# Side-row casts without repeated rows, batch 5 convolved in one phase, and whole side tasks in the first phases of a convolution with a multiplicative feed-forward behind it

## The chip, the cores and the metric

The kernel runs on one core of one Trainium2 chip. TensorE (PE, with its weight loads PEld), VectorE (DVE), ScalarE (ACT) and GpSimd (POOL) compute; SyncE (SP) issues most of the stores and all DMA transpositions; POOL issues the loads that change the type. Each engine works through its own instructions in order. The metric is the device time of one execution in microseconds (us), 539.42 as the median of three runs before the change.

## What is computed

A causal depthwise convolution with 7 taps (softmax weights, one set for each of 8 heads of 24 columns) runs over 8 sequences of 3904 rows and 192 columns; its result goes through a multiplicative feed-forward:

```
w = softmax(weight)                        # 8 heads x 7 taps
y[b, s, h*24+g] = sum_k w[h, k] * xpad[b, s+k, h*24+g]     # six zero rows ahead of each sequence
x  = y.reshape(31232, 192)
a  = x @ w1;  b = x @ w2                   # 192 x 1024 each
out = ((a * b) @ w3) @ w_out               # 1024 x 1024, 1024 x 192
```

The kernel multiplies w3 and w_out once at the start (W_sb, 1024 x 192), so each row needs two products: the first with w1 and w2, the second with W_sb.

## The kernel before, in words

**Rounds and phases.** The 31232 rows are taken as two streams of 15616 rows (NS = 2, four sequences each), and these in 31 rounds of 512 rows (the last one 256). One round does both streams at once: a stream's 64 columns take half of PE's rows. `first_product` (L549) computes for one round eight blocks of 128 features: PE writes `pa` and `pb` (L564), ACT copies `pa` to `asb` (L571), DVE multiplies it with `pb` into `abT` (L573). `second_product` (L583) multiplies `abT` with W_sb (L589), ACT copies the result to `osb` (L594), SP stores it (L599). The main loop (L810) goes in phases, counted from 0 here as in the code: phase p does the first products of one trio of rounds, 3p to 3p+2, then the six second products (n = 0 to 5) of the same trio. Phase 0's first products stand ahead of the loop, with the loads, the W_sb work and the first convolutions between them. So phase 1 holds rounds 3 to 5, phase 4 rounds 12 to 14.

**Two ways to the convolved rows.** Both leave them with columns on partitions.

- The matrix way (17 of the rounds: 0 to 8, 13 to 16, 21 to 24). The input is loaded in windows of 32 rows (`xb`, L158, issued by POOL) in seven batches; batch 3 covers up to round 4, batch 4 rounds 5 to 8, batch 5 rounds 13 to 16, batch 6 rounds 21 to 24. `conv` (L306) multiplies a window with a band matrix on PE (L324), and the result is evicted by ACT or DVE to `convo` (L333). `store` (L340) writes a batch to `rows` in DRAM (SP, L355 and L362), and `transposes` (L392) reads it back transposed to a ring `xT` of four rounds (SP, L396). Batches 4 to 6 are convolved in four units each, a unit being two heads, by `convolve` after one of the second products of a phase; `places` (L694) lists after which. Where a sequence starts inside a batch, POOL clears the six rows ahead of it in `xb` (L831), behind a phase's other POOL work.
- The side way (14 rounds: 9 to 12, 17 to 20, 25 to 30). `side_cast` (L443) copies the input rows of a task (1024 rows, 64 columns, both streams), with 16 rows ahead of them (HALO), to `rows_c` in DRAM in bf16, one DMA on POOL's queue for each stream (L448). `side_transpose` (L454) brings them, columns on partitions, into one of five `raw` tiles in two halves (SP, L457). ACT multiplies the first tap (`side_first`, L462), DVE adds the other six (`side_sums`, L480). Seven half tasks (BY_POOL) are summed by POOL instead (L507, L527, L522), one in each of phases 2 to 8, from a tile that SP transposes (L501) at the end of the phase before.

**The side plan.** The 18 tasks for DVE are dealt to phases in order (L694 to L714): phase p takes sums until `rooms[p]` is used up, so a task may be split over two phases. `starts[p]` are the tasks that begin in phase p; `chain[p]` is the order in which a phase calls `side_first` and the sums, each `side_first` with the earliest n at which it may be emitted. The result before the change: phase 0 does task 0 and three sums of task 1; phase 1 the rest of task 1, task 2, and two sums of task 3; phase 2 the rest of 3, task 4 and one sum of 5; phase 3 the rest of 5 and task 6.

**Order on the queues.** In phase 0 POOL issues (`later_loads`, L735) batch 3's loads, weights, the casts of `starts[0]`, batch 4's loads and the casts of `starts[1]`. SP's order there is: transpositions of `starts[0]`, batch 3's store, xT for rounds 3 and 4 (all L765 and L766), the output stores of the second products, batch 4's store and xT for rounds 5 and 6 (`turn`, L804), the last output store, then the transpositions of `starts[1]`. In the later phases the issues on POOL's queue (`jobs`) are spread over eight points of the first products, each behind a small copy (`pace`, L820) that waits for an `abT` block; a POOL sum stands at seven of these points too. Where a DMA writes rows that an earlier one read, or reads rows that an earlier one wrote, the framework makes it wait.

Of the kernel before, what the change touches and what calls it, by code (L numbers as in the profile page):

```python
# [16 lines left out]
def kernel(  # L17
# [14 lines left out]
    G = D // H  # L32
# [5 lines left out]
    TS = B * S // NS  # L38
# [5 lines left out]
    Q = 64  # L44
# [25 lines left out]
    t0 = (LAG + 3) * CH  # L70
# [26 lines left out]
    def banks(name):  # L97
        return psum.tile([128, NS, CH], FP32, tag="banks", name=name)
# [8 lines left out]
    rows_c = dram.tile([TS, NP, NS * Q], BF16, name="rows_c")  # L107
    taps_d = dram.tile([H, K], FP32, name="taps_d")
    x_rows = x.rearrange("b s d -> (b s) d")


    def shape_of(b):
        n = SIZES[b] // 4
        m = n // (1 if b < 3 else 2)
        return n, m, n // m
# [6 lines left out]
    def group(r, e):  # L122
        return slice((2 * r + e) * C, (2 * r + e) * C + C)
# [55 lines left out]
    for r in range(NS):  # L179
        p = group(r, 0).start  # L180
# [12 lines left out]
        out=diag, in_=diag, pattern=[[-1, 128 + 8]], compare_op=ALU.is_equal,  # L193
# [13 lines left out]
    for i in range(4):  # L207
        d = diag[i * C:i * C + C, i * C + 2 * i:i * C + 2 * i + C]
        nc.vector.tensor_copy(
            out=cmask[i * C:i * C + C],  # L210
            in_=bass.AP(tensor=d.tensor, offset=d.offset, ap=[d.ap[0], [1, 2], [1, C]]))
# [10 lines left out]
    V, A, P = nc.vector.tensor_copy, nc.scalar.copy, nc.gpsimd.tensor_copy  # L222
# [29 lines left out]
    for i in range(3):  # L252
# [3 lines left out]
        out=share[:, :, 0:K], in0=taps.unsqueeze(1).to_broadcast([H, H, K]), scalar=total,  # L256
        in1=diag[0:H, 0:H].unsqueeze(2).to_broadcast([H, H, K]), op0=ALU.mult, op1=ALU.mult)
    spread = banks("spread")
    for i in range(4):
# [6 lines left out]
        out=wsb, in_=spread[:, 0, 0:2 * H].rearrange("p (h k) -> p h k", h=H)  # L266
# [5 lines left out]
        out=cprod.rearrange("p h k (s two) -> p h k s two", two=2),  # L272
# [6 lines left out]
    p = group(1, 0).start  # L279
# [3 lines left out]
    for k in range(2):  # L283
# [5 lines left out]
                          in_=bps[:, 0, 0:C * H].rearrange("p (h s) -> p h s", s=C))  # L289
# [8 lines left out]
    def segments(c0, n):  # L298
        out = []
        while n:  # L300
            m = min(n, Q - c0 % Q)
            out.append((c0 // Q, c0 % Q, m))
            c0, n = c0 + m, n - m
        return out

    def conv(b, c0, wd, evict=(nc.scalar.copy,), es=None):  # L306
        n, m, E = shape_of(b)
        es = range(E) if es is None else es
        if b not in convo_of:
            convo_of[b] = work.tile([128, n, NP, NS, Q], BF16, tag="convo", bufs=2,  # L310
                                    name="convo")
            left_of[b] = D * E
        convo = convo_of[b]
        cps = {e: banks("cps") for e in es}
        c = c0
        while c < c0 + wd:
            h = c // G
            c1 = min(h * G + G, c0 + wd)
            for j in range(4):
                xb, s = xb_of[b][j]  # L320
                for e in es:
                    for r in range(NS):
                        o = cps[e][j * C:j * C + C, r, 0:m * wd]
                        nc.tensor.matmul(  # L324
                            o.rearrange("p (w g) -> p w g", g=wd)[:, :, c - c0:c1 - c0],
                            Aband[group(r, e), h, :], xb[group(r, e), s:s + m, c:c1],
                            start=True, stop=True)
            c = c1
        for f, e in zip(evict, es):
            src = cps[e][:, :, 0:m * wd].rearrange("p r (w g) -> p r w g", g=wd)  # L330
            o = 0
            for k, lo, c in segments(c0, wd):
                f(out=convo[:, e::E, k, :, lo:lo + c]  # L333
                    .rearrange("p w r g -> p r w g"), in_=src[:, :, :, o:o + c])
                o += c
        left_of[b] -= wd * len(es)
        if not left_of[b]:
            del xb_of[b]
# [61 lines left out]
    HALO = 16  # L400
# [15 lines left out]
    def half_of(q, h):  # L416
        t0, t1 = side_span(q)
        return t0 + h * CH, min(t0 + h * CH + CH, t1)
# [3 lines left out]
    for q in SIDE:  # L422
        for k in range(NP):
            left = [h for h in range(2) if (q, k, h) not in BY_POOL]
            if left:
                tasks.append((q, k, half_of(q, left[0])[0], half_of(q, left[-1])[1]))
    side_of, acc_of, raw_of = {}, [], []
    RAW = HALO + 2 * CH

    def side_tiles():  # L430
# [12 lines left out]
    def side_cast(i, task=None):  # L443
        p, k, t0, t1 = task or tasks[i]

        def job(r):
            def run():
                nc.gpsimd.dma_start(  # L448
                    out=rows_c[t0 - HALO:t1, k, r * Q:r * Q + Q],
                    in_=x_rows[r * TS + t0 - HALO:r * TS + t1, k * Q:k * Q + Q])  # L450
            return run
        return [job(r) for r in range(NS)]

# [6 lines left out]
    def side_first(i):  # L460
        p, k, t0, t1 = tasks[i]
        nc.scalar.activation(  # L462
            out=acc_of[i % 2][:, 0:t1 - t0], in_=raw_of[i % 5 - 1][:, HALO - 1:HALO - 1 + t1 - t0],
            func=ACT.Copy, scale=wC[:, k, K - 2:K - 1])

    def side_sums(i):
        p, k, t0, t1 = tasks[i]
        starts = [z for z in range(0, TS, S) if t0 <= z < t1]
        o = t0 - side_span(p)[0]

        def job(d, last):
            def run():
                raw, acc = raw_of[i % 5 - 1], acc_of[i % 2]
                if d == 2:
                    for z in starts:
                        nc.vector.memset(acc[:, z - t0:z - t0 + 1], 0.0)
                for lo, hi in [(t0, t1)] if last else \
                        zip([t0] + [z + d for z in starts], starts + [t1]):
                    a = acc[:, lo - t0:hi - t0]
                    nc.vector.scalar_tensor_tensor(  # L480
                        out=side_of[p][:, k, o:o + t1 - t0] if last else a,
                        in0=raw[:, HALO + lo - t0 - d:HALO + hi - t0 - d],
                        scalar=wC[:, k, K - 1 - d:K - d], in1=a, op0=ALU.mult, op1=ALU.add)
            return run
        size = (t1 - t0) / (2 * CH)
        return [(size, job(d, d == 0)) for d in list(range(2, K)) + [0]]
# [204 lines left out]
    def stage_of(R):  # L691
        return R // TRIO

    places = {0: (1, 2, 3, 4), 2: (1, 3), 3: (0, 1), 4: (2, 4), 5: (1, 3)}  # L694
    rooms = (9, 11, 11, 11, 11, 12, 12, 12, 12)
    starts, chain, room, p = {}, {}, 0, -1
    for i, (q, *_) in enumerate(tasks):
        for cost, f in side_sums(i):
            while room < cost:
                p += 1  # L700
                room = rooms[p]
                at, ends = 0, {}
                starts.setdefault(p, [])
            if not chain or chain[max(chain)][-1][0] != i:
                starts[p].append(i)
                n = max((p == 0) * (3 * len(starts[p]) - 2), -(-ends.get(i - 2, 0) // 2))
                chain.setdefault(p, []).append((i, n, lambda i=i: side_first(i)))
            assert p < stage_of(2 * q + 1)
            room, at = room - cost, at + cost
            chain.setdefault(p, []).append((i, None, f))  # L710
        ends[i] = at
# [62 lines left out]
    jobs = {p: [] for p in range(1, len(phases))}  # L774
# [4 lines left out]
    casts = [(p - 1, f) for p in starts if p > 1 for i in starts[p] for f in side_cast(i)]  # L779
# [3 lines left out]
    for p in jobs:  # L783
        due_now = sum(d <= p for d, _ in casts)
        ahead = max(due_now, min(len(casts), len(points) - len(jobs[p])))
        first = [] if p == 1 else [f for _, f in casts[:due_now]]
        jobs[p] = first + jobs[p] + [f for _, f in casts[len(first):ahead]]
        del casts[:ahead]
    sent = [LAG + 3]
    due = []  # L790

    def convolve(p):
        b, h, n = units.pop(0)
        conv(b, h * G, n * G, (V, A) if p not in chain or (p == 0 and h == 2 * n) else (A, A))
        if h + n == H:
            store(b)
            while sent[0] < len(conv_rounds) and \
                    min((conv_rounds[sent[0]] + 1) * CH, TS) <= spans[b - 3][1]:
                due.append(conv_rounds[sent[0]])
                sent[0] += 1  # L800
            if p == 0:
                turn(0)

    def turn(p):  # L804
        while due and stage_of(due[0]) <= p + 2 and \
                stage_of(conv_rounds[ring_of[due[0]] - RING // CH]) <= p:
            transposes(due.pop(0))

    pace = const.tile([1, 2], BF16)
    for p, (rounds, ends) in enumerate(phases):  # L810
# [3 lines left out]
        at = [[todo.pop(0) for _ in range(min(each, len(todo)))] for _ in points]  # L814
# [29 lines left out]
        for n, (R, r) in enumerate((R, r) for R in ends for r in range(NS)):  # L844
            (last_product if (R, r) == (NR - 1, NS - 1) else second_product)(R, r)
            if n in places.get(p, ()):
                convolve(p)
            side_steps(p, n + 1, state)
# [35 lines left out]
```

## Time and profile before

| what | value |
|---|---|
| runs | 538.75, 539.42, 539.61 us; median 539.42 |
| the profiled execution | 539.89 us, of which its span (first to last instruction) 538.2 us |
| PE busy | 512.4 us, 95% of the span; granted clock 0.974 in the mean |
| DVE, ACT, POOL busy | 444.7, 348.8, 230.6 us |
| DMA | 58.50 MB, 109 GB/s in the mean |

The page also cuts the span in 40 equal slices of 13.45 us; a digit is the busy share in tenths, and PEclk the granted clock of TensorE:

```
PE   9999699399999999994999999999999999999997
PEclk 9999889789999999996999999999999999999999
DMA  9999959975945496599923636897741320040024
```

PE's row has three low digits inside the run: the fifth slice (53.8 to 67.3 us), the eighth (94.2 to 107.6) and the nineteenth (242.2 to 255.6). The phases of the main loop begin, by PE's first L564 matmul of each, at 77.65, 135.70, 183.81, 231.92, 290.05, 338.10, 385.29 and 432.48 us; phase 0's second products begin at 52.58.

### The profile page before, as it was taken

What the parts mean: (1) busy time and instruction counts of PE and PEld (TensorE: products, weight loads), DVE (VectorE), ACT (ScalarE), POOL (GpSimd) and SP (SyncE); (2) the same over time, 40 slices, a digit from 0 to 9 for tenths busy, and PEclk for the clock granted to TensorE, in tenths of its full rate; (3) what the DMA queues carried; (4) which work ended last, traced back from release to release, by engine and by line L of the source; (5) the groups of instructions that cost most, each with busy time, mean ns of one, the idle gap of its engine ahead of it and who ended that gap; (6) DMA issues with size and microseconds to landing.
All of it is one profiled execution on the core that took longest, in us unless ns stands there. A gap on an engine that the chain in (4) does not pass through costs nothing.

```text
span 538.2 us, 13687 instructions
## 1 busy us (share of the span) xinstructions
PE 512.4 (95%) x5764; PEld 342.5 (64%) x5764; DVE 444.7 (83%) x396; ACT 348.8 (65%) x389; POOL 230.6 (43%) x301
## 2 busy tenths in 40 slices
PE   9999699399999999994999999999999999999997
PEld 4447575159557755951587559557755955775597
DVE  7898289479899799982997999899999999999940
ACT  6786377263776677561767776676477467647742
POOL 8866203100496099335731890395088037300000
PEclk9999889789999999996999999999999999999999
DMA  9999959975945496599923636897741320040024
GB/s 139 152 150 177 108 116 233 169 142 137 152 53 93 128 90 71 113 155 179 144 72 118 50 22 133 147 157 109 202 39 14 119 75 2 31 148 1 1 62 147
DMA packets 157273, 58.50 MB, mean 109 GB/s; under 512 B 113055, under 2 KB 157211, under 8 KB 157211
## 3 DMA queue, kind: packets, MB, share of 16 engines
q0 software_dynamic: 71008, 16.90, 34.7%
q1 hardware_dynamic: 86043, 40.62, 32.5%
q8 instruction: 45, 0.74, 0.5%
q14 instruction: 17, 0.14, 0.1%
q10 hardware_dynamic: 160, 0.10, 0.1%
HBM read 34.09 MB, written 34.90 MB: 128 GB/s over the span
## 4 chain that ended last, share of the span: by engine, by line
PE 77%; DMA 11%; POOL 4%; DVE 3%; SPq 1%; ACT 1%; issue 1%; POOLq 0%; ACTq 0%; DVEq 0%
PE ops L589 26%; PE pa L564 25%; PE pb L564 25%; DMA xb<-in_x_dram 3%; DVE acc L480 2%; DMA rows_c<-in_x_dram 2%; DMA xT<-rows 2%; DMA rows<-convo 2%; POOL xb L158 1%; POOL ws L220 1%; POOL w3b L638 1%; DMA wn<-in_moe_w_dram 1%; SPq L362 1%; PE cps L324 1%; SPq L396 1%
## 5 line engine op out<-in xcount | busy, mean ns | idle before, releaser
L573 DVE TENSOR_TENSOR abT<-asb,pb 128x1024 bf16<-128x1024 bf16 x240 | 292.5, 1220 | 54.8 <-ACT asb L571 21.0
L571 ACT CAST asb<-pa 128x1024 bf16<-128x1024 f32 x244 | 247.1, 1013 | 85.4 <-PE pa L564 85.1
L564 PEld LDWEIGHTS <-wn 64*128 64x128 bf16 x1488 | 138.9, 95 | 96.1 <-DMA xT<-rows 15.9
L564 PEld LDWEIGHTS <-ws 64*128 64x128 bf16 x1488 | 129.9, 94 | 73.3 <-issue 6.1
L589 PE MATMUL ops<-W_sb,abT 128*128 128x192 bf16 x1936 | 165.2, 247 | 0.2 <-ACT convo L333 0.2
L589 PEld LDWEIGHTS <-abT 128*128 128x128 bf16 x1936 | 159.9, 98 | 7.0 <-issue 6.8
L564 PE MATMUL pa<-xT,wn 64*128 64x512 bf16 x408 | 113.1, 383 | 16.1 <-DMA xT<-rows 16.0
L564 PE MATMUL pb<-xT,wn 64*128 64x512 bf16 x408 | 113.6, 381 | 0.0
L564 PE MATMUL pa<-xT,ws 64*128 64x512 bf16 x408 | 113.2, 383 | 0.0
L564 PE MATMUL pb<-xT,ws 64*128 64x512 bf16 x408 | 110.3, 381 | 0.1
L594 ACT COPY osb<-ops 128x768 f32<-128x768 f32 (+1 forms) x61 | 48.5, 795 | 84.4 <-PE ops L589 82.6
L820 POOL COPY pace<-abT 1x2 bf16<-1x2 bf16 x56 | 9.8, 175 | 191.6 <-DVE abT L573 172.6
L564 PE MATMUL pb<-side,wn 64*128 64x512 bf16 (+1 forms) x336 | 88.9, 368 | 0.1
L564 PE MATMUL pa<-side,wn 64*128 64x512 bf16 (+1 forms) x336 | 87.3, 369 | 0.0
L564 PE MATMUL pa<-side,ws 64*128 64x512 bf16 (+1 forms) x336 | 87.3, 369 | 0.0
L480 DVE SCALAR_TENSOR_TENSOR acc<-raw,wC,acc 128x1024 f32<-128x1024 bf16 (+2 forms) x70 | 85.1, 1216 | 2.5 <-ACT acc L462 0.5
L564 PE MATMUL pb<-side,ws 64*128 64x512 bf16 (+1 forms) x336 | 85.6, 368 | 0.0
L507 POOL TENSOR_SCALAR tmp<-acc,wC 128x512 f32<-128x512 bf16 x42 | 65.9, 1568 | 1.2
L448 POOL DMA_DIRECT2D rows_c<-in_x_dram x50 | 38.0, 763 | 22.2 <-DMA raw<-rows_c 16.6
L527 POOL TENSOR_TENSOR acc<-acc,tmp 128x512 f32<-128x512 f32 x35 | 44.4, 1268 | 2.9
L158 POOL DMA_DIRECT2D xb<-in_x_dram x50 | 32.6, 657 | 7.2 <-DMA xb<-in_x_dram 4.0
L480 DVE SCALAR_TENSOR_TENSOR acc<-side,wC,acc 128x1024 f32<-128x1024 bf16 (+1 forms) x20 | 25.2, 1261 | 11.2 <-ACT acc L462 10.7
(71 smaller groups left out, 188.8 us busy)
## 6 DMA issues: line engine op xcount, KB each, us to landing
out_dram<-osb SPq DMA_DIRECT2D x54, 384.0 KB
xb<-in_x_dram POOLq DMA_DIRECT2D x16, 240.0 KB, 7.5
rows_c<-in_x_dram POOLq DMA_DIRECT2D x28, 130.0 KB, 5.3
out_dram<-osb SPq DMA_DIRECT2D x12, 192.0 KB
rows<-convo SPq DMA_DIRECT2D x6, 240.0 KB
xb<-in_x_dram POOLq DMA_DIRECT2D x6, 228.0 KB, 5.5
rows_c<-in_x_dram POOLq DMA_DIRECT2D x16, 66.0 KB, 3.4
w3b<-in_moe_w_dram POOLq DMA_DIRECT2D x4, 256.0 KB, 5.0
```

Of the source, the lines that this page charges most:

```text
L158: nc.gpsimd.dma_start(out=tiles[js[0]][0][group(r, e), s:s + w, :], in_=bass.AP(tensor=x.tensor, offset=(r * TS + t - PAD) * D, ap=[[D, C] ...
L220: f(out=wsw[k][Q * h:Q * h + Q, lo:hi], in_=wn[k][Q - Q * h:2 * Q - Q * h, lo:hi])
L448: nc.gpsimd.dma_start(out=rows_c[t0 - HALO:t1, k, r * Q:r * Q + Q], in_=x_rows[r * TS + t0 - HALO:r * TS + t1, k * Q:k * Q + Q])
L480: nc.vector.scalar_tensor_tensor(out=side_of[p][:, k, o:o + t1 - t0] if last else a, in0=raw[:, HALO + lo - t0 - d:HALO + hi - t0 - d], sc ...
L507: nc.gpsimd.tensor_scalar(out=out, in0=pool_raw[0][:, HALO - d:HALO - d + CH], scalar1=wC[:, k, K - 1 - d:K - d], scalar2=None, op0=ALU.mult)
L527: nc.gpsimd.tensor_tensor(out=a, in0=a, in1=tmp[:, lo - t0:hi - t0], op=ALU.add)
L564: nc.tensor.matmul(p[:, r, f * N:f * N + N], w_of(i, k, r)[rs, ft * 128:(ft + 1) * 128], operand(R, k, rs), start=(k == 0), stop=(k == NP ...
L571: nc.scalar.copy(out=asb[:, :, 0:per * N], in_=pa[:, :, 0:per * N])
L573: nc.vector.tensor_tensor(out=ab[:, f0, :, 0:N], in0=asb[:, :, 0:N], in1=pb[:, :, 0:N], op=ALU.mult)
L589: nc.tensor.matmul(ops[:, g // 2, (g % 2) * D:(g % 2) * D + D], ab[:, jt, r, g * 128:(g + 1) * 128], W_sb[:, jt, :], start=(jt == 0), stop ...
L594: nc.scalar.copy(out=osb.rearrange("p (a g) d -> p a (g d)", g=2), in_=ops[:, 0:ng // 2, 0:2 * D])
L820: P(out=pace, in_=abT_of[R][0:1, ft, 1, 0:2])
```

## The change

Five edits, all in how work is ordered:

- A cast starts at its own first row, without the 16 rows ahead of it, where an earlier cast of the same columns and stream ended at that row (`cast_to`).
- `rooms` goes from 9, 11, 11, 11 to 6, 12, 12, 12 in the first four phases. Whole tasks result: phase 0 does task 0; phase 1 tasks 1 and 2; phase 2 tasks 3 and 4; phase 3 tasks 5 and 6. Task 1's casts and transpositions move from `starts[0]` to `starts[1]`, task 3's from `starts[1]` to `starts[2]`.
- `places`: batch 5's four units stand after n = 0, 1, 3, 4 in phase 2, not after 1, 3 of phase 2 and 0, 1 of phase 3. Its store, which follows the last unit, moves with them, and the xT of rounds 13 and 14 to the end of phase 2.
- A `side_first` may be emitted from about half the sums ahead of it in its phase, less one: n = 2 for the second task.
- `jobs`: in each phase batch loads stand ahead of casts (before: the casts due stood first, but in phase 1). In phase 0 the first half of the third and the fourth unit of batch 4 is evicted by DVE (before: of the third only).

```diff
-    side_of, acc_of, raw_of = {}, [], []
+    side_of, acc_of, raw_of, cast_to = {}, [], [], set()
...
         def job(r):
             def run():
+                lo = t0 if (t0, k, r) in cast_to else t0 - HALO
+                cast_to.add((t1, k, r))
                 nc.gpsimd.dma_start(
-                    out=rows_c[t0 - HALO:t1, k, r * Q:r * Q + Q],
-                    in_=x_rows[r * TS + t0 - HALO:r * TS + t1, k * Q:k * Q + Q])
+                    out=rows_c[lo:t1, k, r * Q:r * Q + Q],
+                    in_=x_rows[r * TS + lo:r * TS + t1, k * Q:k * Q + Q])
...
-    places = {0: (1, 2, 3, 4), 2: (1, 3), 3: (0, 1), 4: (2, 4), 5: (1, 3)}
-    rooms = (9, 11, 11, 11, 11, 12, 12, 12, 12)
+    places = {0: (1, 2, 3, 4), 2: (0, 1, 3, 4), 4: (2, 4), 5: (1, 3)}
+    rooms = (6, 12, 12, 12, 11, 12, 12, 12, 12)
...
-                n = max((p == 0) * (3 * len(starts[p]) - 2), -(-ends.get(i - 2, 0) // 2))
+                n = max(p == 0, int(at) // 2 - 1, -(-ends.get(i - 2, 0) // 2))
...
         ahead = max(due_now, min(len(casts), len(points) - len(jobs[p])))
-        first = [] if p == 1 else [f for _, f in casts[:due_now]]
-        jobs[p] = first + jobs[p] + [f for _, f in casts[len(first):ahead]]
+        jobs[p] += [f for _, f in casts[:ahead]]
...
-        conv(b, h * G, n * G, (V, A) if p not in chain or (p == 0 and h == 2 * n) else (A, A))
+        conv(b, h * G, n * G, (V, A) if p not in chain or (p == 0 and h >= 2 * n) else (A, A))
```

## The prediction

> **What bounds the kernel now.** I read the slices of the page first: PE is busy 95% of the span, and only three slices away from the start fall under 9 tenths. So a change can gain what PE loses there and no more. Next I cut the span at the phase borders (the first pa matmul of each phase) and asked for the busy time of each engine in each stretch. Columns: stretch, length, then busy time of PE, PEld, DVE, ACT, POOL with counts, granted clock, DMA share, GB/s.
>
> ```profile
> 52.58:77.65 25.07, 19.98 (x324) 17.88 (x322) 13.59 (x13) 12.46 (x18) 4.02 (x7) 0.86 0.89 113
> 77.65:135.70 58.05, 49.47 (x483) 31.85 (x484) 43.80 (x36) 31.15 (x32) 7.95 (x15) 0.91 1.00 171
> 135.70:183.81 48.11, 48.11 (x546) 32.72 (x548) 43.75 (x35) 34.65 (x38) 27.96 (x34) 1.00 0.61 101
> 231.92:290.05 58.13, 50.75 (x546) 32.41 (x548) 43.26 (x35) 34.71 (x38) 28.07 (x32) 0.91 0.85 142
> 385.29:432.48 47.19, 47.19 (x483) 32.44 (x484) 44.42 (x39) 31.59 (x33) 22.48 (x24) 1.00 0.34 70
> ```
>
> The last row is a full phase without a convolution: 47.19 us, PE never idle. The third has two convolution units: 0.92 more, so a unit costs PE 0.46. Against these, phase 1 (second row) is 58.05 - 47.19 = 10.86 us too long and phase 4 (fourth row, two units) 58.13 - 48.11 = 10.02. The first row holds only the second products of phase 0. Six such products without a convolution took 15.95 us (385.29 - 369.34, in the chain), four units add 1.84, and 25.07 - 17.79 = 7.28 us is lost. In all 28.2 us.
>
> The view of who waited for whom (us in total, times, longest) and the chain that ended last (start, us, what) name the causes:
>
> ```profile
> PE pa L564 <- DMA xT<-rows: 16.0, 3, 8.6
> PE cps L324 <- ACT osb L594: 4.4, 1, 4.4
> ACT acc L462 <- DMA side<-rows_c: 7.4, 1, 7.4
> POOL rows_c L448 <- DMA raw<-rows_c: 16.6, 1, 16.6
> ```
> ```profile
> 55.35 5.55 DMA rows_c<-in_x_dram
> 60.96 2.56 DMA side<-rows_c
> 63.63 1.15 ACT acc L462
> ...
> 67.23 4.28 PE ops L589 x32
> ...
> 89.13 10.96 DMA rows<-convo
> 100.11 6.97 DMA xT<-rows
> ```
>
> In phase 0, ACT stands at L462 until side task 0 is transposed. The second half of that transposition leaves SP at 60.96, when the cast in flight from 55.35 has landed: the cast of task 3, whose 16 halo rows (5616 to 5631, same columns) are the last rows of task 0. Behind ACT's wait stand the evictions, so PE stands too. Phase 1's loss is the wait of round 5 for batch 4's rows, stored late; phase 4's is round 13's wait for batch 5's. SP's timeline shows why batch 4 is late (start, time, line, operation, count):
>
> ```profile
> 64.80 4.93 SPq L362 DMA_DIRECT2D rows<-convo  x8
> 70.34 8.68 SPq L396 DMA_TRANSPOSE xT<-rows  x6
> 79.06 4.45 SPq L599 DMA_DIRECT2D out_dram<-osb  x5
> 83.61 10.40 SPq L362 DMA_DIRECT2D rows<-convo  x6
> ...
> 223.48 7.69 SPq L362 DMA_DIRECT2D rows<-convo  x6
> ```
>
> All of this stands in one queue behind the transposition held to 60.96. The evictions for the first store had ended at 49.74.
>
> **The change part by part.**
>
> *Halo rows left out, task 1 out of phase 0.* Task 0's second transposition now depends on its own casts alone (the built program lists only an older transposition's semaphore there) and can follow the first, issued at 44.12: lands by about 45.3 + 1.3 + 2.6 = 49.2. ACT reaches L462 after its first osb, at 56.24, so 7 us of cover lie over it. Six sums (6 x 1.27) and the two units whose first half DVE now evicts (2 x 1.21) fit in DVE's stage, which holds nine sums now; each sum too many would cost 1.27. Gain: 7.28; phase 1 starts at 70.4. The halo rows themselves are 16 of 1040: nothing. On POOL task 1's two casts move behind batch 4's twelve loads, so these come some 2 us earlier; task 3's two casts move to phase 1.
>
> *Batch 4's store.* SP no longer stands from 45.3 to 60.96, nor issues task 1's two transpositions first. The first store starts at 49.8. It and the six xT transpositions took 64.80 to 79.02, 14.3 us; started at 49.8 that is 64.1, or 67.2 if batch 4's loads slow them as much as phase 1's loads and casts slowed batch 4's store (15.85 us, 83.61 to 99.46, against 12.96 for batch 5's, 223.48 to 236.44: a factor of 1.22). Five output stores follow at 0.89 each, but the fifth waits for the fifth second product (52.58 + 5 x 2.66 + 3 x 0.46 = 67.3) and its eviction (0.80), ready at 68.2, and batch 4's last unit is evicted at 67.7 + 1.2 = 68.9. So the store starts between 69.2 (68.2 and one output store) and 71.7 (67.2 and five). From its start to round 5's first matmul it was 107.12 - 83.61 = 23.5 us; with batch 5's faster store 20.6. Round 5 can start between 89.8 and 95.2. PE wants it two rounds (77.65 to 98.4) after 70.4, at 91.1. A stall of 0 to 4.1 is left, and with it up to 1.4 of slow clock (the stall of 4.4 us was followed by products of 4.28 for 2.75). I take the middle, 92.5: 1.4 of stall and 0.6 of clock, 2.0. Gain: 10.86 - 2.0 = 8.9.
>
> *All four units of batch 5 in phase 2.* PE does the same matmuls. The store's twelve DMAs (13 us of SP) move from phase 3 to the end of phase 2, ahead of one output store, for which nobody waits; then rounds 13 and 14 are transposed (9 us), so xT is there some 25 us before phase 4. Gain: 10.0. ACT gets two more units in phase 2 (3.7 us) and two fewer in phase 3; it is busy 34.65 of 48.11. The new wait is on POOL: the first unit now follows the first second product and needs the zero rows before a sequence's start (L831), which POOL writes after its side sums, and phase 2 has one pair of DMA issues more (seven, as phase 3 has now):
>
> ```profile
> 169.36 0.56 POOL L831 MEMSET xb<- 6x192 bf16 x2
> 219.09 0.56 POOL L831 MEMSET xb<- 6x192 bf16 x2
> ```
>
> Six pairs: done at 169.92, 34.22 after the phase began. Seven pairs: 219.65 - 183.81 = 35.84. PE reaches the unit at 166.94 - 135.70 + 2.75 = 33.99. So PE waits 1.85, with five second products and their evictions behind it. Slow clock after it: between 0 and 1.85/4.4 of 1.53, 0.6; I take 0.3, since the wait is under half the shortest one that the rows show. Cost 2.2. [...]
>
> *Casts behind the loads, whole tasks.* In phases 2 to 4 the casts go out three points later. Their transpositions serve sums a phase later, some 50 us of cover. Phases 1 to 3 get 12 sums of DVE instead of 11; phase 7 (last row above) already has 12 and loses nothing; without that cover each sum is 1.27. Phase 1's first task is now transposed behind batch 4's store, but 3 us or more before the second products; if that cover went, ACT would wait at L462 as in phase 0, where 7.4 cost PE 7.3. POOL's 16.6 us wait (a cast over rows that task 2's transposition still reads) goes too; nothing on PE hung on it.
>
> Sum: 539.89 (the profiled execution; its span is 538.2) - 7.28 - 8.86 - 10.02 + 2.15 = 515.9. The profiled execution is 0.47 over the median of 539.42, so 515.4; I say 515.5.
>
> **Rivals.**
>
> *Nothing left over:* round 5 finds its tiles and the zero rows come in time: 539.4 - 28.2 = 511.2. For it: the low bounds above. Against it: seven pairs on POOL took what they took.
>
> *The store moves into the loads' time and crawls.* From 49.8 the first store and six transpositions share the DMA engines with the last of batch 4's loads and four casts, and the DMA share from 52.58 on is already 0.89. If this takes all that SP has won, round 5's loss stays whole: 511.2 + 10.86 + 2.2 = 524.3. For it: batch 4's store, 22% slower beside such traffic. Against it: 22% of 14.3 is 3.1, and the last of these loads is issued at 52.42 already. [...]
>
> *The change does not free the transposition:* the rows of tasks 1 and 2 are the same rows in other columns. If these count as an overlap, phases 0 and 1 stay as they are: 539.4 - 10.0 + 2.2 = 531.6. Against it: the built program's waits.
>
> *Slower:* POOL's order in phase 2. A cast ahead of the zero rows that waits on a transposition, as in the 16.6 us row, holds the memset, PE's unit and all second products behind it. One such wait makes 511.2 + 16.6 + 2.2 = 530, two make 546.6. It decides from 28.2 - 2.2 = 26 us of delay on. For it: casts and loads share POOL's queue. Against it: the rows that made that wait are the halo that is left out.
>
> **How the numbers follow.** Forecast 0.67, nothing left over 0.11, crawling store 0.14, transposition not freed 0.04, slower 0.03, a sum that cancels 0.01. Range 510.5 to 524.5: from just under the floor of 511.2 over the unknown costs (up to 5.5 for round 5, 2.5 for POOL: 519.2) to the crawling store. A measurement of this kernel can tell about 0.2% (1.1 us) from no change. Faster 0.96, within 0.01, slower 0.03.
>
> **What would show it.** Phase 0's second products take about 17.8 and ACT no longer waits at L462; the second transposition of task 0 stands right behind the first; phase 1 is 47.2 to 52.7 long; phase 2 is about 51, with PE waiting on the zero rows; phase 4 is 48.1 and no wait on xT is left there. The forecast is wrong if round 5 waits over 6 us, if ACT waits at L462 in phases 1 to 3, or if DVE delays the first pa eviction of a phase.

## The result and the profile after

| | before | after |
|---|---|---|
| median of four runs | 539.51 us | 525.76 us (524.77 to 527.28) |
| ratio after to before | | 0.9739, interval 0.9697 to 0.978 |
| profiled execution, its span | 539.89, 538.2 us | 525.93, 524.2 us |
| PE busy, granted clock | 512.4 us, 0.974 | 509.9 us, 0.990 |

The change gains 13.8 us, where 24 were predicted, and ends just above the predicted range. The same cut at the phase borders as before says where (stretch, length, busy time of PE, PEld, DVE, ACT, POOL, granted clock, DMA share, GB/s; after):

```profile
52.98:70.70 17.72, 17.72 (x321) 16.28 (x322) 11.45 (x11) 10.61 (x16) 1.81 (x4) 1.00 1.34 137
70.70:129.02 58.32, 50.85 (x483) 32.10 (x484) 43.27 (x35) 31.15 (x32) 7.88 (x15) 0.91 1.05 176
129.02:180.26 51.24, 49.44 (x611) 32.05 (x610) 47.20 (x37) 38.28 (x44) 29.61 (x36) 1.00 0.62 95
180.26:227.40 47.14, 47.14 (x483) 31.33 (x482) 43.23 (x35) 31.15 (x32) 29.51 (x36) 1.00 1.21 165
227.40:276.07 48.67, 48.46 (x547) 32.64 (x548) 45.99 (x37) 34.72 (x38) 28.80 (x32) 1.00 0.64 101
```

Four of the five rows came as forecast: phase 0's second products 17.72 (17.8), phase 2 51.24 (about 51; 52.95 in a second profile), phase 3 47.14, phase 4 48.67 (48.1). Phase 1 is the miss: 58.32, where 49.2 was forecast (47.19 and a residue of 2.0) and 58.05 stood before. With 0.4 by which phase 0's second products begin later and 0.6 in phase 4, the 9.1 make up the 10.0 between the forecast sum of 515.9 and 525.93.

The view of who waited for whom, after, has what is left on PE, and the chain that ended last shows phase 1's part of it (start, us, what):

```profile
PE pa L566 <- DMA xT<-rows: 7.5, 3, 6.6
PE cps L324 <- POOL xb L832: 1.8, 1, 1.8
```
```profile
92.30 7.93 DMA xT<-rows
100.24 0.04 issue
100.28 0.61 PE pa L566 x2
100.89 1.28 PE pb L566 x6
102.17 1.28 PE pa L566 x6
103.45 1.28 PE pb L566 x6
104.73 1.22 PE pa L566 x6
105.95 0.65 PE pb L566 x6
```

Round 5 waits 7.5 us in three pieces, and six matmuls then take 1.28 us instead of 0.65 until about 105.9: half clock (granted clock 0.50 from 98.30 to 105.70). PE's busy time has it, 50.85 - 47.19 = 3.7 us. Together these are phase 1's 11.1 (58.32 - 47.19). ACT's wait for the side tile of task 0 (7.4 us before) is gone. SP's timeline, after, shows why round 5 is late although SP no longer stands until 60.96:

```profile
43.41 2.51 SPq L459 DMA_TRANSPOSE side<-rows_c  x2
50.14 5.65 SPq L362 DMA_DIRECT2D rows<-convo  x8
57.82 11.56 SPq L396 DMA_TRANSPOSE xT<-rows  x6
69.43 4.44 SPq L601 DMA_DIRECT2D out_dram<-osb  x5
73.98 9.21 SPq L362 DMA_DIRECT2D rows<-convo  x6
83.23 0.42 SPq L355 DMA_DIRECT2D rows<-convo  x1
83.70 2.96 SPq L362 DMA_DIRECT2D rows<-convo  x4
88.09 0.24 SPq L355 DMA_DIRECT2D rows<-convo  x1
89.01 10.29 SPq L396 DMA_TRANSPOSE xT<-rows  x6
```

The first store starts 14.7 us earlier than before, batch 4's only 9.6 (73.98 for 83.61), and the six xT transpositions of rounds 3 and 4 took 11.56 us for 8.68. From 89.01 it is 9.2 us to round 5's first matmul (98.21) and 11.3 to its third tile (100.28); before it was 7.0 from 100.11 to the first.

### The profile page after: what moved, and what is told of

Its sections match the earlier page's. It is cut to its first block, busy times and chain, and to the rows that moved or that the text cites. A ratio compares the mean times of both kernels' runs of the same rounds, so it can differ in the third digit from the quotient of the medians.

```text
span 524.2 us, 13679 instructions
## 1 busy us (share of the span) xinstructions
PE 509.9 (97%) x5764; PEld 340.0 (65%) x5764; DVE 447.1 (85%) x397; ACT 347.9 (66%) x388; POOL 231.0 (44%) x301
## 4 chain that ended last, share of the span: by engine, by line
PE 83%; POOL 7%; DVE 4%; ACT 2%; DMA 2%; issue 1%; SPq 0%; POOLq 0%; DVEq 0%
PE ops L591 27%; PE pa L566 27%; PE pb L566 26%; DVE acc L482 3%; POOL tmp L509 2%; DVE abT L575 2%; DMA xT<-rows 2%; POOL xb L158 1%; PE cps L324 1%; POOL acc L529 1%; ACT asb L573 1%; PE wps L659 1%; POOL rows_c L450 1%; ACT convo L333 0%; PE ops L612 0%
## 5 line engine op out<-in xcount | busy, mean ns | idle before, releaser
L575 DVE TENSOR_TENSOR abT<-asb,pb 128x1024 bf16<-128x1024 bf16 x240 | 292.3, 1221 | 43.0 <-ACT asb L573 17.4
L482 DVE SCALAR_TENSOR_TENSOR acc<-raw,wC,acc 128x1024 f32<-128x1024 bf16 (+2 forms) x70 | 86.7, 1239 | 3.2 <-ACT acc L464 1.2
L333 ACT CAST convo<-cps 128x640 bf16<-128x640 f32 (+2 forms) x47 | 28.1, 668 | 4.0 <-PE cps L324 3.9
```

The lines of the kernel that those rows point to most:

```text
L333: f(out=convo[:, e::E, k, :, lo:lo + c] .rearrange("p w r g -> p r w g"), in_=src[:, :, :, o:o + c])
L482: nc.vector.scalar_tensor_tensor(out=side_of[p][:, k, o:o + t1 - t0] if last else a, in0=raw[:, HALO + lo - t0 - d:HALO + hi - t0 - d], sc ...
L575: nc.vector.tensor_tensor(out=ab[:, f0, :, 0:N], in0=asb[:, :, 0:N], in1=pb[:, :, 0:N], op=ALU.mult)
```

## The experiments

Every kernel ran beside the kernel before on the same chip; its medians in the five sets lay between 538.1 and 539.9, so ratios are compared. The last columns are lengths in one profiled execution each, which isn't always a typical one: of "outputs behind the store" it was the fastest of four (520.92, the others up to 527.7), of "combined, but outputs ahead" the slowest (517.03, the others up to 513.71).

| kernel | median us | ratio [interval] | phase 1 | phase 2 |
|---|---|---|---|---|
| changed kernel, again | 525.0 | 0.9733 [0.9708, 0.9758] | 54.9 | 53.0 |
| POOL held in phase 1 | 520.14 | 0.9658 [0.9626, 0.9689] | 49.7 | 53.7 |
| only casts held | 521.03 | 0.9653 [0.9628, 0.9678] | 52.2 | 52.9 |
| only loads held | 521.71 | 0.9674 [0.9646, 0.9702] | 52.6 | 53.0 |
| tasks 1, 2 cast in phase 1 | 526.08 | 0.9768 [0.9739, 0.9798] | 60.2 | 51.2 |
| halo rows cast again | 522.39 | 0.9695 [0.9653, 0.9736] | 53.9 | 53.0 |
| outputs behind the store | 524.47 | 0.9756 [0.971, 0.9802] | 51.3 | 53.7 |
| raw tiles ahead of xT(6) | 525.36 | 0.9726 [0.9697, 0.9754] | 55.8 | 52.9 |
| these two together | 517.31 | 0.9592 [0.9559, 0.9625] | 51.0 | 51.3 |
| zero rows early | 521.37 | 0.9655 [0.9628, 0.9683] | 56.4 | 49.0 |
| the three orders, POOL in place | 513.67 | 0.9534 [0.949, 0.9578] | 47.3 | 49.0 |
| combined, but outputs ahead | 513.7 | 0.953 [0.9496, 0.9564] | 51.9 | 49.0 |
| combined | 511.96 | 0.949 [0.9466, 0.9513] | 47.1 | 49.0 |
| combined, halo rows cast again | 512.02 | 0.9481 [0.9449, 0.9514] | 47.1 | 49.0 |
| before, first edit alone | 532.89 | 0.987 [0.9852, 0.9889] | 51.4 | 48.1 |
| before, side plan alone | 529.86 | 0.9805 [0.9775, 0.9834] | 54.4 | 49.2 |
| before, places alone | 529.04 | 0.9795 [0.9769, 0.9821] | 57.8 | 49.3 |

### Is it POOL's traffic that round 5 shares its way with?

POOL's issues of phase 1 (batch 5's first loads, casts of tasks 3 and 4 and of a POOL half) are held until round 5's blocks:

```diff
+        pts = points if p != 1 else tuple((2, v) for v in range(8))
...
-                              for v, (a, ft) in enumerate(points) if a == j and at[v]})
+                              for v, (a, ft) in enumerate(pts) if a == j and at[v]})
```

> The changed kernel, but what POOL issues in phase 1 (batch 5's first loads, the casts of tasks 3 and 4 and one POOL half) is held until round 5's own blocks; the order on SP is untouched. Theory (sharing): round 5 is late because batch 4's store and the xT transpositions share the DMA engines with POOL's loads and casts. Then batch 4's store falls from 14.4 us towards the 13.0 of batch 5's, the time from the first xT issue to round 5's full speed from 11.3 towards 7.0, and the whole is some 5 us faster than the changed kernel: 519 to 522. Rival (SP's line): the time is set by what stands in SP's queue in order, whatever else is moved. Then nothing changes: 525 to 527.

The ratio falls from 0.9733 to 0.9658. SP's work is the same and in the same order, and round 5's tiles come sooner: store at 73.01, first xT of round 5 at 86.74, third tile 7.3 us behind it instead of 11.3. PE waits 2.2 us for them, and no half clock follows (granted clock 1.00 in phase 1). So the traffic of POOL's queue slowed a transposition of SP's here, and the late place of the store on SP's queue is not the whole of it. The DMA view of the stretch from the first xT of round 5 to its last wait on PE (queue, packets, MB, busy share of the engines), in the changed kernel and in this one, shows POOL's queue (q0) gone beside SP's (q1):

```profile
q0 software_dynamic: 5106, 0.71, 103.1%
q1 hardware_dynamic: 2865, 0.98, 72.4%
```
```profile
q1 hardware_dynamic: 1980, 0.63, 55.6%
```

But new waits appear; ACT's and PE's timelines of this kernel:

```profile
107.66 1.15 ACT L464 ACTIVATE acc<-raw,wC 128x1024 f32<-128x1024 bf16 x1 [3.08 <-DMA xb<-in_x_dram]
111.56 1.15 ACT L464 ACTIVATE acc<-raw,wC 128x1024 f32<-128x1024 bf16 x1 [1.16 <-DMA raw<-rows_c]
```
```profile
125.72 0.37 PE L566 MATMUL pb<-xT,wn 64*128 64x512 bf16 x1 [2.25 <-DVE abT L575]
```

The raw tiles of tasks 1 and 2, transposed behind everything else on SP's queue, are now what is late: ACT stands at L464, DVE's sums end late, and PE pays 2.25 us for it. (The profile puts the first of ACT's two waits down to a load, but the instruction reads only a raw tile.)

Loads or casts alone (the points `pts` of phase 1 are `((0, 1), (0, 4))` and then round 5 for the casts; or `((0, 7), (1, 2), (1, 5))` for the casts, which then stand ahead of the loads in the list, and then round 5 for the loads):

> The changed kernel itself, as the base for the three kernels beside it on the same chip. Ratio to the kernel before 0.974 to 0.977, as in the first runs; round 5's wait for xT in three pieces, 16 to 18 us in all, phase 1 58 us long, and PE's wait of 1.75 us for the zero rows in phase 2.

> The changed kernel with only the three pairs of casts of phase 1 (tasks 3, 4 and the POOL half) held to round 5's blocks; batch 5's two pairs of loads stay at 75.7 and 79.6 us, beside batch 4's store. Theory A (the casts, which run beside xT(5) and xT(6), are what slows the transpositions): xT of round 5 takes 7.0 to 7.5 us from first issue to third tile instead of 11.3, round 5 waits 2 to 4 us, phase 1 is 51 to 53 us long and the ratio to the kernel before 0.966 to 0.969, as where all issues were held. Theory B (the loads, which run beside the store and push it back, cost the time): the store still ends at 88 and the transpositions still take 11 us; 58 us, ratio 0.974 to 0.977. Both halves alike: in between, 54 to 56 us and 0.970 to 0.973.

> The opposite: the changed kernel with only batch 5's two pairs of loads of phase 1 held to round 5's blocks; the casts stay at 83.5, 87.4 and 91.2 us. Theory A (casts): nothing is gained in the transpositions, third tile of round 5 still 10 us or more after the first issue; the store may end up to 1 us earlier (13.6 for 14.35); phase 1 56 to 58 us, ratio 0.972 to 0.977. Theory B (loads): 51 to 53 us, ratio 0.966 to 0.969.

In the total neither theory wins: each half alone brings what both bring together (0.9653 and 0.9674, intervals overlapping). SP's and PE's timelines show why. With the casts held, the store still takes 14.4 us (73.41 to 87.80), but from the first xT of round 5 to its last wait on PE it is 6.4 us (88.47 to 94.84). With the loads held, the store takes 13.6 (71.64 to 85.23), but the tiles 9.7 (85.32 to 95.01). By these profiles, one each, the casts slowed the transpositions, and the loads the store. That round 5 is complete at the same time is in part chance: the store of the second kernel began 1.8 us earlier, before anything differs between the two. The changed kernel's two profiles show how wide this spread is. The same six transpositions of rounds 3 and 4 took 11.56 us of SP in the first and 8.38 in the second, of which these are lines of SP and PE:

```profile
57.88 8.38 SPq L396 DMA_TRANSPOSE xT<-rows  x6
66.31 4.71 SPq L601 DMA_DIRECT2D out_dram<-osb  x5
71.11 8.79 SPq L362 DMA_DIRECT2D rows<-convo  x6
87.40 9.44 SPq L396 DMA_TRANSPOSE xT<-rows  x6
```
```profile
94.31 0.60 PE L566 MATMUL pa<-xT,wn 64*128 64x512 bf16 x1 [2.96 <-DMA xT<-rows]
97.01 0.58 PE L566 MATMUL pa<-xT,ws 64*128 64x512 bf16 x1 [2.09 <-DMA xT<-rows]
```

So that profile has waits of 5.05 us for round 5, not the 16 to 18 that were expected, and phase 1 lost 7.7 us (54.91 - 47.19), not 11.1.

The opposite, more casts into phase 1 (casts of tasks 1 and 2 out of phase 0, to the first points of phase 1; further lines, not shown, keep their transpositions in place on SP's queue):

```diff
-        for i in starts[1]:
-            for f in side_cast(i):
-                f()
...
+    jobs[1] = [f for i in starts[1] for f in side_cast(i)] + jobs[1]
```

> The changed kernel, but the casts of tasks 1 and 2 leave phase 0 and are the first that POOL issues in phase 1; SP's order is the same. Sharing: the six xT transpositions of rounds 3 and 4 fall from 11.6 us to about 9, batch 4's store starts 2.5 us earlier, but then has the casts beside it: 522 to 526. SP's line: 525 to 527.

The transpositions of rounds 3 and 4 take 8.04 us and the store starts at 70.86; with the casts in place these were 11.56 and 73.98 in one profile, but 8.38 and 71.11 in the other, so a gain there isn't shown. Then the six of rounds 5 and 6 take 13.44 (10.29 and 9.44 before) and round 5 waits 9.3 us. Beside them now run four loads of batch 5, issued from 83.14 to 87.60 and landed from 91.41 to 101.11, and two casts. So it wasn't the casts as such that slowed the transpositions here, but what was in flight on POOL's queue at that time. Ratio 0.9768, no gain.

### What are the halo rows worth?

```diff
-                lo = t0 if (t0, k, r) in cast_to else t0 - HALO
+                lo = t0 - HALO
```

> The changed kernel with the 16 halo rows cast again. Theory: the new rooms alone free task 0's transposition, since no task whose halo lies in task 0's rows and columns is cast in phase 0 any more; only POOL's last cast pair of phase 1 waits again (16 us, for which nothing on PE waits): 525 to 527. Rival: leaving the rows out is what freed it; then ACT waits at its first side multiplication again and phase 0's second products take 25 us, not 17.7: 533 or more.

Not slower than the changed kernel: 0.9695, with intervals that overlap; 522.39 us is under the 525 to 527 that were expected. Task 0's transposition stays free, so the first edit isn't needed for that. POOL's timeline, of this kernel, shows what the halo does in phase 1:

```profile
86.70 0.17 POOL L821 COPY pace<-abT 1x2 bf16<-1x2 bf16 x1 [1.58 <-DVE abT L575]
101.90 1.51 POOL L450 DMA_DIRECT2D rows_c<-in_x_dram  x2 [15.02 <-DMA raw<-rows_c]
```

Task 4's casts wait 15 us for a raw transposition over the same rows, and so stay out of the way of round 5's tiles until these are there. In the changed kernel the same pair goes out at 87.37. But the loads and casts issued before, from 79.41 to 84.33, landed only from 88.27 to 94.37, and from the first xT of round 5 to its last wait it took 9.6 us, as in the changed kernel's second profile. That this wait gains time isn't shown.

The edits alone, on the kernel before (the first: the lines on `cast_to`; the second and fourth: the lines on `rooms` and `n`; the third: the line `places`, all as in the change):

> The kernel before with the first edit alone (casts leave out the 16 rows that an earlier cast has brought). My account: SP no longer stands until 60.96, the 7.3 us of phase 0's second products come back, batch 4's store starts some 10 us earlier; but POOL's wait of 16.6 us goes too, so that the casts of phase 1 run beside the transpositions of rounds 5 and 6, and phase 1 keeps 5 to 11 us of its loss; phase 4 keeps its 10 us. Ratio to the kernel before 0.976 to 0.987. If the halo rows cost nothing beside the transposition that they hold (my prediction): phase 1 falls to 49 us and the ratio is 0.970 or less. If they were not what held it: nothing changes, ratio 1.

> The kernel before with the second and fourth edit alone (whole tasks, task 1 out of phase 0). If the new deal alone frees task 0's transposition (task 3's cast is no longer in flight then): phase 0's second products take 17.8 us instead of 25.1, batch 4's store starts 9 to 12 us earlier, phase 1 is 51 to 57 us, phase 4 keeps its 10 us: ratio to the kernel before 0.970 to 0.981. If phase 0 needs the first edit for it: phase 0 keeps 23 us or more, ratio 0.987 or more. Phase 2 has seven pairs of issues on POOL now, but its unit comes after the second second product, so no wait for zero rows.

> The kernel before with the third edit alone (all four units of batch 5 in phase 2). My account: phase 4 falls from 58.1 to 48.1 us, phase 2 grows by two units, 0.92, and by PE's wait of 1.75 us for the zero rows, with or without 1.66 us of half clock behind it; phase 3 loses the two units, 0.92. Phases 0 and 1 stay. 539.7 - 10.0 + 1.75 = 531.4, or 533.1 with the slow clock: ratio 0.983 to 0.989. If the two edits lean on each other (the gain of phase 4 needs the casts behind the loads): less than 4 us gained, ratio above 0.992.

The first edit alone frees the transposition, but phase 0's second products still take 24.6 us. PE's timeline of that kernel names another wait there, for batch 4's own loads, which share the stretch (DMA share 1.45) with the casts of four tasks and the freed store:

```profile
61.33 0.27 PE L324 MATMUL cps<-xb,Aband 32*32 32x240 bf16 x1 [2.05 <-DMA xb<-in_x_dram]
62.98 0.59 PE L324 MATMUL cps<-xb,Aband 32*32 32x240 bf16 x21 [1.38 <-DMA xb<-in_x_dram]
```

The side plan alone brings phase 0 to 17.8, as expected: taking task 3's casts out of phase 0 is enough. A wait of 0.84 us for the zero rows in phase 2, where none was expected, is new there. Places alone brings phase 4 from 58.1 to 48.06, better than expected, since PE loses only 0.3 us to the zero rows (the unit takes 0.73 us instead of 0.42): with the old side plan POOL has six pairs of issues in phase 2, not seven, and the zero rows are written at 169.36 for a unit at 169.63. So the wait that the prediction put down to the places needs the new plan too. The three gains, 0.013, 0.0195 and 0.0205, add up to 0.053; the change has 0.026 of it. The plan and the places, less 0.008 for the zero rows (next), make 0.032, and the kernel with the halo cast again has 0.0305: the first edit adds nothing to them.

### What do the zero rows cost, and what follows a short wait?

```diff
+        if p == 2:
+            at[5].insert(0, clear)
```

(`clear`, defined above these lines, does the memsets of L832.)

> The changed kernel with one edit: the zero rows of batch 5 are cleared at the sixth point of phase 2's first products. PE's 1.75 us wait in phase 2 goes, and with it the 1.66 us of half clock that followed it in five of nine profiled executions: phase 2 is 49.0 us long; 1.75 to 3.4 us below the changed kernel, ratio to the kernel before 0.967 to 0.971. Phase 1 keeps its 55 to 58 us. If the wait was only the last of several (ACT or DVE late at the same place): ratio 0.972 or more.

0.9655 for 0.9733, some 4 us with an uncertainty of about 2, where 1.75 to 3.4 were expected; phase 2 is 48.98 us long, 4.0 less than in the changed kernel's second profile. PE's timeline after the same wait, in the first profile of the changed kernel and in the second:

```profile
164.94 0.69 PE L324 MATMUL cps<-xb,Aband 32*32 32x240 bf16 x22 [1.75 <-POOL xb L832]
165.57 2.81 PE L591 MATMUL ops<-W_sb,abT 128*128 128x192 bf16 x32
```
```profile
161.36 0.69 PE L324 MATMUL cps<-xb,Aband 32*32 32x240 bf16 x22 [1.75 <-POOL xb L832]
161.98 4.47 PE L591 MATMUL ops<-W_sb,abT 128*128 128x192 bf16 x32
```

Equal waits, and 1.66 us more for the next product in one of them. Where the wait lay in each execution stands in the last section.

### The orders on SP's queue, and all together

Phase 0's output stores behind batch 4's store and its transpositions (`held` collects them, the end of `convolve` in phase 0 issues them):

```diff
+            held.append(send) if holding[0] else send()
...
             if p == 0:
                 turn(0)
+                holding[0] = False
+                for f in held:
+                    f()
```

> The changed kernel, but phase 0's first five output stores go to SP behind batch 4's store and the transpositions for rounds 5 and 6. SP's line: batch 4's store starts 4.4 us earlier (69.5 for 74.0) and round 5 too: 521 to 522. Sharing: the store starts earlier as well, but its time and that of the transpositions grows where the loads and casts of phase 1 come beside it: a gain of 2 to 4.4, 521 to 524. This run alone does not tell them apart; it prices the output stores that stand ahead.

The raw tiles of tasks 1 and 2 between xT(5) and xT(6), no longer behind the last output store:

```diff
             if p == 0:
+                transposes(due.pop(0))
+                for i in starts[1]:
+                    side_transpose(i)
                 turn(0)
...
-        for i in late:
+        for i in late if p else ():
```

> The changed kernel with one edit on SP's queue: the four transpositions of tasks 1 and 2 stand between xT(5) and xT(6). If xT(6) right behind slows xT(5) (two sets of transpositions into the same streams): the third tile of round 5 comes 8 to 9 us after the first issue instead of 11 to 13, phase 1 is 2 to 5 us shorter, ratio to the kernel before 0.964 to 0.969. If any traffic behind it is alike: round 5 comes as late as before, 0.972 to 0.976. If xT(6) now comes too late for its round: a new wait on xT(6) and 0.976 or more.

> The changed kernel with two edits on SP's queue that each gained nothing alone: the output stores behind batch 4's store and its transpositions, and the transpositions of tasks 1 and 2 between xT(5) and xT(6). POOL is as in the changed kernel, the zero rows too. If the two gain only together (the store must be early, and the raw tiles must not fall behind the output stores): phase 1 is 47 to 49 us, phase 2 keeps its wait of 1.7 us and, by chance, 1.66 us of half clock, and the ratio to the kernel before is 0.957 to 0.964. If what the kernel with early zero rows gained beside them hung on the zero rows: 0.970 or more.

Alone each gains nothing (0.9756, 0.9726), together 0.014 (0.9592): with the outputs behind, the store starts at 69 instead of 71 to 74, but the raw tiles fall behind six stores, unless they go first. That xT(6) right behind slows xT(5) isn't borne out: with the raw tiles there in its place, round 5 still waited 5.8 us.

All of it, with POOL held too (the combined kernel), and two kernels that leave one part of it out:

> The changed kernel with four moves together: phase 1's POOL issues held to round 5's blocks; phase 0's five output stores behind batch 4's store and its transpositions; the transpositions of tasks 1 and 2 put between xT(5) and xT(6); and batch 5's zero rows cleared at the sixth point of phase 2's first products instead of behind them. If the explanation (shared DMA engines for round 5, POOL's order for the zero rows, ACT's wait for late raw tiles as what appeared when the POOL issues were held) is whole: round 5 waits under 1 us, ACT does not wait at L464, phase 1 is 47.5 to 49 us, phase 2 49.1 to 49.6, and the ratio to the kernel before is 0.951 to 0.957 (511.5 to 515 us). If the raw transpositions ahead of xT(6) push it past its round: a wait of some 3 us moves from round 5 to round 6, and the ratio is 0.958 to 0.962. If the zero rows are not what PE waited for, phase 2 keeps its 51 us.

> The combined kernel without its hold on POOL: output stores behind batch 4's store, the transpositions of tasks 1 and 2 between xT(5) and xT(6), early zero rows, but phase 1's loads and casts at their old points beside the store and the transpositions. If sharing with POOL's traffic costs time of itself: the store and the three transpositions of round 5 together take 3 to 5 us longer than the 17.2 us of the combined kernel (69.0 to 86.2), round 5 comes at 90 to 94 and may wait up to 3 us; the raw tiles and xT(6) behind it come later too, and the ratio to the kernel before is 0.953 to 0.963. If the earlier place of the store on SP's queue was all that was needed: 0.947 to 0.952, as the combined kernel.

> The combined kernel with phase 0's five output stores ahead of batch 4's store again, as in the changed kernel; POOL's issues stay held. If what round 5 has left over beside the hold is SP's place: the store starts at 73 instead of 69.0, round 5's third tile is there at 93.5 to 94.5, PE waits 1.5 to 3 us for it in phase 1 and no more, and the ratio to the kernel before is 0.952 to 0.956. If the hold alone carries the gain: 0.947 to 0.952.

> The combined kernel with the 16 halo rows cast again. POOL then waits at task 4's casts for the raw tile's transposition, but in round 5's blocks and later, where no transposition that PE waits for is in flight. If the first edit is worth nothing once round 5 is out of the way: ratio to the kernel before 0.947 to 0.952, as the combined kernel. If the wait on POOL delays batch 5's loads or POOL's sums of phase 2: PE waits at L324 or ACT at L464, and 0.953 or more.

The combined kernel, cut at its phase borders, and SP's timeline:

```profile
70.29:117.43 47.14, 47.14 (x483) 31.12 (x482) 43.22 (x35) 31.14 (x32) 7.63 (x15) 1.00 1.00 151
117.43:166.40 48.97, 48.97 (x609) 31.66 (x610) 46.40 (x37) 38.17 (x44) 31.69 (x36) 1.00 0.97 156
```
```profile
69.00 7.66 SPq L362 DMA_DIRECT2D rows<-convo  x6
...
81.21 4.94 SPq L396 DMA_TRANSPOSE xT<-rows  x3
86.32 5.78 SPq L459 DMA_TRANSPOSE raw<-rows_c  x4
92.20 3.82 SPq L396 DMA_TRANSPOSE xT<-rows  x3
96.06 8.19 SPq L604 DMA_DIRECT2D out_dram<-osb  x6
```

PE loses nothing in phases 1 and 2 any more, at a granted clock of 1.00. 511.96 us is 27.7 less than before, of the 28.2 that the prediction counted as lost. Leaving out the hold on POOL or the early store costs about 0.004 each, but the intervals overlap that of the combined kernel, so neither price is shown; single runs of these two reach 518.2 and 517.0, while the combined kernel stays within 0.4 us. So with SP's orders changed, POOL's traffic is mostly hidden in three runs of four. The halo rows make no difference (0.9481).

## Why the prediction was wrong, point by point

- *What bounds the kernel* was right: 28.2 us in three places, and the combined kernel gets 27.7 of them back.
- *Phase 0, 7.28, and phase 4, 10.02:* right, to 0.1 and 0.6 us. But the reason named for phase 0 was half right: the whole-task plan is enough to free the transposition; leaving out the halo rows alone frees it too, but exchanges its wait for one on batch 4's loads.
- *The step that failed:* "I take the middle, 92.5: 1.4 of stall and 0.6 of clock, 2.0. Gain: 10.86 - 2.0 = 8.9." Phase 1 lost 11.1 us, and 7.7 in the second profile. Round 5 came at 98.21, above the upper end of 95.2. The store started at 73.98, not between 69.2 and 71.7 (71.11 in the second profile), since the first store and its six transpositions took 19.2 us (50.14 to 69.38), over the 17.4 allowed for; from there to round 5's first matmul it took 24.2, over the 23.5 of the upper end; and the half clock cost 3.7 where I had 0.6. In the second profile round 5's first matmul came at 94.31, inside the range, and the step failed all the same: a later tile of the round was late by another 2.09, which the sum has no term for, and the half clock cost 2.6 (PE busy 49.76 - 47.19). The factor 1.22 was taken from a store beside loads and casts; the transpositions were never costed beside them (7.0 us before, 11.3 and 9.6 here), and the trace of before couldn't show it, because POOL stood 16.6 us there and its queue moved only 0.16 MB in those 7.0 us.
- *"The halo rows themselves are 16 of 1040: nothing"* and *"nothing on PE hung on it"* (that 16.6 us wait) hang together. The wait kept the casts away from the transpositions that PE waits for: with the first edit alone they took 12.1 us (88.80 to 100.86), for 7.0 before. What that costs isn't shown: the kernel with the halo rows is not slower, nor is it shown to be faster.
- *Zero rows, 2.15:* right in the profiled execution (51.24 for phase 2) and 1.7 short in the second (52.95), so luck in part: the 0.3 for the clock was a mean of two cases, 0 and 1.66. Taking the wait away gained some 4 us, give or take 2.
- *The rival of the crawling store* (524.3, chance 0.14) comes nearest in number and has part of the mechanism. The first store and its six transpositions did slow down, by 4.9 us of the 14.7 that SP had won (19.2 for 14.3; 16.4 in the second profile). The rest was lost in phase 1, beside loads and casts that the rival doesn't name. I argued against it that the factor was worth 3.1 us and that batch 4's loads end at 52.42; the casts of tasks 1 and 2, issued behind them, and phase 1's traffic were left out of that argument.

## What to carry to other kernels

A wait that seems to cost nothing may be what keeps a transfer out of another's way (round 5's first transpositions took 7.0 us with POOL's 16.6 us wait, 12.1 with the first edit alone): before removing it, look at what will then start, and which transposition on another queue runs at that time. When several orders on a queue gain nothing one by one, try them together, since the next tile in line takes the place of the one that was freed. Cost a stall that is left as the waits for all tiles of a round and the half clock behind them (7.5 and 3.7 us here), and forecast an arrival from the slowest row, not from the middle, where a late arrival pays twice.

## What the runs showed of the hardware

After a wait of PE of 1.69 to 1.76 us (the zero rows), the granted clock fell to one half in six of ten profiled executions with that wait and stayed full in four. One-us stretches of the changed kernel's second profile (columns as above):

```profile
162.06:163.06 1.00, 1.00 (x11) 0.98 (x12) 0.96 (x2) 0.94 (x2) 0.00 (x0) 0.76 0.74 155
162.56:163.56 1.00, 1.00 (x10) 0.95 (x8) 0.96 (x2) 1.00 (x2) 0.00 (x0) 0.51 0.78 208
165.56:166.56 1.00, 1.00 (x40) 0.82 (x38) 0.96 (x2) 0.07 (x1) 0.00 (x0) 0.79 0.00 0
```

At 0.76 and 0.79 the clock is full for about half of each of these stretches, so it fell near 162.6, over 1 us after PE was at work again, and rose near 166.0: 3.4 us.

Where the wait lay decided it in each execution in which it can be counted. The granted clock in the profile before changes at 63.49, 70.32, 101.04, 111.28, 244.40 and 254.64 us (one us around each has 0.75): 2, 9, 3, 39 and 3 times 3.413 us from one to the next. In the first profile of the changed kernel it changed at 95.53 and 105.77 (3 times), in the second at 94.31, 101.14, 162.57 and 165.98 (2, 18 and 1). So the half clock lasted 3.41, 6.83 or 10.24 us in these three. In the second profile the step of 3.41 us that ended at 162.57 began at 159.16, and the wait lay whole inside it, from 159.61 to 161.36. In the first, 20 steps after 95.53 is 163.80, inside the wait (163.19 to 164.94), so 0.61 us of it lay in one step and 1.14 in the next. In other profiles the steps can be counted from where round 5's matmuls return to full speed, to about 0.2 us:

| kernel | full speed from | border, us | wait, us | clock after it |
|---|---|---|---|---|
| halo rows cast again | 100.1 | 158.1 and 161.5 | 158.57 to 160.33 | half |
| raw tiles ahead of xT(6) | 102.4 | 160.5 and 163.9 | 160.72 to 162.41 | half |
| outputs behind the store | 97.5 | 155.6 and 159.0 | 156.64 to 158.33 | half |
| these two together | 97.7 | 155.8 | 155.38 to 157.09 | full |
| tasks 1, 2 cast in phase 1 | 107.3 | 165.3 | 164.64 to 166.34 | full |

In the first profiles before and after the change, the clock fell at the ends of steps in which PE stood 2.36 (63.49), 2.50 (101.04), 2.02 (244.40) and 3.41 us in all (95.53); steps after the change with 0.52, 0.61 and 1.20 us left it full. So the zero rows cost 1.7 us, or 1.66 more, by how the wait lay to these steps, and that differed from run to run. A wait of 1.87 us up to 93.38 (POOL held, phase 1) left the clock full; the granted clock of phases 1 and 2 is 1.00 in that profile, with no change to count from, so it isn't shown why.

With traffic on POOL's queue, transpositions of SP's took longer in these runs. From the first xT of round 5 to its last wait on PE it took 6.4 to 7.7 us where that queue moved 0.16 MB or less (casts held 6.4; before 7.0; POOL held 7.3; side plan alone 7.4; combined, but outputs ahead 7.7), 9.1 and 9.6 us with 0.40 and 0.44 MB (places alone; halo rows cast again), and 9.6 to 15.2 us with 0.52 to 1.11 MB in nine other profiles. A longer stretch also lets more through, so the amounts alone don't show the direction; the kernels in which only POOL's issues were held do (7.3 and 6.4 us, for 11.3 and 9.6 in the changed kernel). How the DMA engines divide their time between the two queues isn't shown by any run here.
